# First head pair of a causal attention turned by halves of the tokens

## The chip, the cores and the metric

One core of a Trainium2 chip runs the whole program. The metric is device time in microseconds (us) of one execution. Engines: TensorE (PE, with its weight loads as PEld), VectorE (DVE), ScalarE (ACT), GpSimd (POOL) and SyncE (SP), which issues the DMAs.

## What is computed

```python
def reference(**kwargs):
    ...
    attn_out = _attn_ref(**attn_kwargs)          # q, k, v: (2, 12, 448, 64) float32
    x = np.ascontiguousarray(attn_out.transpose(0, 2, 1, 3)).reshape(B * S, H * D)
    x = _moe_ref(x=x, **moe_kwargs)              # (silu(x @ w_gate) * (x @ w_val)) @ w_out
    return _moe2_ref(x=x, **moe2_kwargs)         # h = x @ w_in; (h * clip(h + 3, 0, 6) / 6) @ w_out

def _attn_ref(q, k, v):
    scores = scale * np.matmul(q, k.transpose(0, 1, 3, 2))
    mask = np.triu(np.ones((seq, seq), dtype=bool), k=1)
    scores = np.where(mask, -1000000000.0, scores)
    scores = scores - np.max(scores, axis=-1, keepdims=True)
    attn = np.exp(scores)
    attn = attn / (np.sum(attn, axis=-1, keepdims=True) + 1e-09)
    return np.matmul(attn, v).astype(np.float32)
```

## The kernel before

`attention()` takes the 24 heads as 12 pairs; the two heads of a pair lie side by side on the 128 rows of a tile (2 x 64). Tokens are cut into four chunks of 112. After the attention, `mlps()` runs the two gated layers, which take the rest of the span.

For one pair, q and k come into `nat` tiles, are turned so that the head's 64 numbers lie along the rows, and are split into a rounded part and a remainder (`qh`, `ql`, `kh`, `kl`; the products are three matmuls, kh with qh, kl with qh and kh with ql). Pairs 0 and 1 (`BY_PE = 2`) are turned on TensorE, four transposes for q and four for k (tiles `tr`); ACT then copies the rounded part out (`CAST kh<-tr`) and DVE subtracts it for the remainder (`kl<-tr,kh`). The later pairs are turned on DVE (`STREAM_TRANSPOSE f<-nat`) and split on POOL, ACT and DVE.

Scores (`sc`) are made in groups of query chunks, `GROUPS = ((2,), (0, 1), (3,))`: chunk c needs keys 0 to c only, so it is (c + 1) x 112 wide, with 224 as the least. DVE adds the mask, scales and takes the extreme value (`e<-sc,mask`, with `m`), ACT takes the exponential (`e<-e,m`) with its row sum, TensorE turns the exponentials (`tp`, ten transposes a head), ACT or DVE copies them out (`et`), and TensorE multiplies them with v (`pv`).

The order on each engine is not written by hand. Every step is handed to a `Plan` (`op`) with a cost per engine that may do it, with what it reads and writes; `Plan.run` then places the steps one by one by their earliest start and by due times worked back from the sum of TensorE's costs. A step with several possible engines is placed on one of them there. The program order that comes out is kept on every engine, so a changed cost, start time (`AT_START`) or step ahead changes the placing of later steps too.

Three places matter below. `load_rows(p)` (L392) issues four loads for pair p on SP, one for each of k and q and each head, 112 rows by four chunks. `busy(n)` issues n matmuls of zeros, 512 columns wide (tile `zero`), which compute nothing that is used; `IDLE = (6, 1, 3, 4)` says how many at the start, after k's turning, after q's, and as filling between the first steps. `first_turn()` (L511) turns pair 0:

```python
for src in (k, q):
    box, parts = rows_turned(0, src)
    got.append(box)
    for part in parts:
        part()
    busy(IDLE[1] if src is k else IDLE[2])
(tk, nk), (tq, nq) = (box["tr"] for box in got)
load(3, k)
load(3, q)
split_bank(0, k, tk, {"act": 0.44})
split_bank(0, q, tq, {"act": 0.44})
```

Of the kernel before, what the change touches and what calls it, by code (L numbers as in the profile page):

```python
# [8 lines left out]
F32 = mybir.dt.float32  # L9
# [5 lines left out]
ALU = mybir.AluOpType  # L15
# [34 lines left out]
BY_PE = 2  # L50
# [2 lines left out]
SOON = 6.0  # L53
CASTS = ("pool", "act")
HOLD, HEAD, LEND = 0.1, 3.0, 0.0
AT_START = {"act": 2.0, "vec": 1.3, "pool": 2.0, "pe": 1.2, "sp": 0.3}
GROUPS = ((2,), (0, 1), (3,))
IDLE = (6, 1, 3, 4)


class InOrder:
# [149 lines left out]
def tile_attention_glu_mlp(  # L211
# [114 lines left out]
    def attention():  # L326
        with ExitStack() as st:
# [21 lines left out]
            def take(kind, n, shape, dt=F32, ready=0.0):  # L349

                i = count[kind] = count.get(kind, -1) + 1
                tag = f"{kind}{i % n}"
                return Spot(lambda: wk.tile(shape, dt, tag=tag, name=kind), (wk, tag), ready=ready)

            def bank(use):
                n = idle.pop(0)
                return Spot(lambda: banks.tile([128, 512], F32, tag=f"bank{n}", name=use), (banks, n)), n
# [3 lines left out]
            def busy(n):  # L361
                for _ in range(n):
                    op(
                        {"pe": 0.38},
                        lambda e: e.matmul(idler(), zeros[:, :128], zeros, start=True, stop=True), writes=[idler],
                    )
# [22 lines left out]
                        writes=[(t, row)], wire=0.6 if rows == 64 else 0.53, soon=SOON,  # L389
                    )  # L390

            def load_rows(p):  # L392

                for src in (k, q):
                    n = (natq if src is q else natk)[p] = take("nat", NAT, [128, NB * D])
                    for j in range(2):
                        op(
                            {"sp": 0.5},
                            lambda e, n=n, j=j, src=src: e.dma_start(
                                out=rows_of(n)[:, :, j, :], in_=src[0, 2 * p + j].rearrange("(c p) d -> p c d", p=C)  # L400
                            ),
                            writes=[(n, j)], wire=0.62,
                        )

            def rows_of(n):
                return n()[:C, : NC * 2 * D].rearrange("p (c j d) -> p c j d", c=NC, j=2)
# [15 lines left out]
            def move(e, out, src):  # L422
                return (e.copy if e.engine is nc.scalar else e.tensor_copy)(out, src)
# [17 lines left out]
            def parts_for(p, src):  # L441
                return sets(p)[:2] if src is q else sets(p)[2:]
# [14 lines left out]
            def split_bank(p, src, t, by):  # L457

                hi, lo = parts_for(p, src)
                op(by, lambda e: move(e, hi(), t()[:, :S]), reads=[t], writes=[hi])  # L460
                op(
                    {"vec": 0.65},
                    lambda e: e.tensor_tensor(out=lo(), in0=t()[:, :S], in1=hi().bitcast(F32), op=ALU.subtract),
                    reads=[t, hi], writes=[lo],
                )

            def rows_turned(p, src):

                n = (natq if src is q else natk).pop(p)
                box = {}  # L470

                def one(c):
                    if c == 0:
                        box["tr"] = bank("tr")
                    op(
                        {"pe": 0.1},
                        lambda e: e.transpose(
                            box["tr"][0]()[:, c * C : (c + 1) * C], rows_of(n)[:, c].rearrange("p j d -> p (j d)"),
                            ident[:C, :C],
                        ),  # L480
                        reads=[n], writes=[box["tr"][0]], kind="tr",
                    )

                return box, [lambda c=c: one(c) for c in range(NC)]
# [25 lines left out]

            def first_turn():  # L511

                got = []
                for src in (k, q):
                    box, parts = rows_turned(0, src)
                    got.append(box)
                    for part in parts:
                        part()
                    busy(IDLE[1] if src is k else IDLE[2])
                (tk, nk), (tq, nq) = (box["tr"] for box in got)  # L520
                load(3, k)
                load(3, q)
                split_bank(0, k, tk, {"act": 0.44})
                split_bank(0, q, tq, {"act": 0.44})
                idle.extend((nk, nq))

            def sc_parts(p):

# [7 lines left out]
                def products(group):  # L536
# [21 lines left out]
                    for cs, terms_ in steps:  # L558
                        op(
                            {"pe": len(terms_) * sum(0.005 + places[c][1] * 0.00044 for c in cs)},  # L560
                            lambda eng, cs=cs, terms_=terms_: work(eng, cs, terms_),
                            reads=[x for i in terms_ for x in terms[i]], writes=[sp for sp, _ in got], kind="sc",
                        )
                    for j, (sp, bn) in enumerate(got):
                        e, m = es[j], ms[j]
# [18 lines left out]
                            )  # L584
                        idle.append(bn)

                return [lambda g=g: products(g) for g in GROUPS]

            def tp_parts(p):

# [203 lines left out]
                    for part in parts:  # L794
                        part()

            for p in range(BY_PE):
                load_rows(p)
            load_v(0)
            load(2, k)  # L800
            load(2, q)
# [825 lines left out]
```

## Time and profile before

| | us |
|---|---|
| median of three runs | 549.36 (549.36, 546.77, 549.46) |
| the profiled execution, whole | 548.23 |
| its span in the profile | 546.5 |
| TensorE busy in it | 536.7 (98%) |
| DVE, ACT, POOL busy | 433.8, 418.8, 196.2 |

The span runs from the first to the last recorded instruction; 1.7 us of the execution lie around it. "Idle before, releaser" in a row names what an engine waited for just before that row. Matmuls overlap, so a row's duration is longer than its distance to the next one. The column PEclk of the stretches is the granted TensorE clock as a share of full speed.

### The profile page before, as it was taken

The numbers are of one execution on the slowest core, as the hardware profiler recorded it, in microseconds if no ns is written. First come the engines' busy times: TensorE is split into PE (matmuls) and PEld (weight loads), VectorE is DVE, ScalarE is ACT, GpSimd is POOL, SyncE is SP. The second block draws the span as 40 slices with busy tenths as digits, with TensorE's granted clock in tenths as the row PEclk, the third lists the DMA queues.
The fourth block names the chain that finished last, engine by engine and source line by source line (L and its number), as shares of the span: only waits on it lengthen the run. The fifth ranks groups of instructions, "written<-read, shape, count | busy, mean of one in ns | idle before, by whom it ended". The sixth has DMA issues, their size and how long they took to land.

```text
span 546.5 us, 8943 instructions
## 1 busy us (share of the span) xinstructions
PE 536.7 (98%) x3107; PEld 486.6 (89%) x3108; DVE 433.8 (79%) x852; ACT 418.8 (77%) x873; POOL 196.2 (36%) x212
## 2 busy tenths in 40 slices
PE   8999999999999999999999999999999999999997
PEld 4677767898999999999999999999999999999997
DVE  5999999899776677699985778777767867599983
ACT  5999986768878778589879877898887847686550
POOL 1798997403232342232020154432333610000511
PEclk9999999999999999999999999999999999999999
DMA  7987713155454544311015444534541066510112
GB/s 204 252 224 213 149 59 116 59 175 172 130 197 137 172 132 158 117 58 59 1 59 185 146 129 122 170 115 132 163 170 58 1 176 215 186 58 2 58 44 101
DMA packets 60236, 69.31 MB, mean 127 GB/s; under 512 B 16928, under 2 KB 54048, under 8 KB 60192
## 3 DMA queue, kind: packets, MB, share of 16 engines
q1 hardware_dynamic: 60192, 68.76, 41.6%
q8 instruction: 24, 0.39, 0.3%
q14 instruction: 20, 0.16, 0.1%
HBM read 65.99 MB, written 2.75 MB: 126 GB/s over the span
## 4 chain that ended last, share of the span: by engine, by line
PE 84%; DVE 11%; DMA 2%; POOL 1%; ACT 1%; issue 1%; POOLq 0%
PE mm L70 73%; PE sc L70 4%; PE pv L70 3%; PE tp L70 3%; DVE op L70 2%; DVE out L70 1%; DVE w L70 1%; PE tr L70 1%; DMA raw<-in_moe_w_gate_dram 1%; DVE e L70 1%; PE zero L70 1%; DVE v L70 1%; DVE et L70 1%; DVE ws L70 1%; DVE t L70 1%
## 5 line engine op out<-in xcount | busy, mean ns | idle before, releaser
L70 PE MATMUL mm<-x,a 128*128 128x448 f32 x396 | 86.3, 365 | 0.0
L70 PE MATMUL mm<-x,s 128*128 128x448 f32 x378 | 81.0, 365 | 0.0
L70 PEld LDWEIGHTS mm<-x,a 128*128 128x128 f32 x396 | 74.4, 188 | 5.9
L70 PEld LDWEIGHTS mm<-x,s 128*128 128x128 f32 x378 | 71.0, 188 | 5.6
L70 ACT ACTIVATE raw<-raw,half 128x768 uint32<-128x768 uint8 x64 | 63.9, 1001 | 0.0
L70 PE MATMUL mm<-t,s 128*128 128x448 f32 x270 | 58.2, 366 | 1.3 <-ACT mm L70 1.3
L70 PE MATMUL mm<-op 128*128 128x384 f32 x315 | 56.6, 335 | 0.3 <-DVE out L70 0.3
L70 PEld LDWEIGHTS mm<-t,s 128*128 128x128 f32 x270 | 50.6, 188 | 5.7 <-ACT mm L70 1.7
L70 PEld LDWEIGHTS mm<-op 128*128 128x128 f32 x315 | 54.7, 188 | 0.9 <-ACT op L70 0.6
L70 ACT ACTIVATE e<-e,m 112x224 f32<-112x224 f32 (+3 forms) x96 | 49.7, 538 | 3.1 <-DVE m L70 3.1
L70 POOL TENSOR_TENSOR a<-w,a 128x384 fp32r<-128x384 f32 x22 | 23.4, 1062 | 72.1 <-ACT a L70 71.3
L70 PE MATMUL mm<-go,wo 128*128 128x448 f32 x189 | 38.9, 366 | 0.0
L70 DVE SCALAR_TENSOR_TENSOR v<-v,raw 128x768 uint32<-128x768 uint32 x34 | 33.9, 1000 | 6.0 <-ACT raw L70 5.9
L70 PEld LDWEIGHTS mm<-go,wo 128*128 128x128 f32 x189 | 35.4, 188 | 3.2 <-ACT mm L70 0.4
L70 ACT ACTIVATE w<-raw 128x768 f32<-128x768 f32 x34 | 31.0, 911 | 8.4 <-DMA raw<-in_moe_w_out_dram 5.5
L70 DVE CUSTOM_DVE_ANT_0 e<-sc,mask 112x112 f32<-112x112 f32 (+3 forms) x96 | 36.5, 437 | 1.1 <-PE sc L70 1.1
L70 DVE SCALAR_TENSOR_TENSOR w<-w,raw 128x768 uint32<-128x768 uint32 x30 | 29.0, 968 | 10.2 <-ACT raw L70 10.2
L70 ACT COPY tmp<-mm 128x448 f32<-128x448 f32 x45 | 23.8, 532 | 12.8 <-PE mm L70 12.5
L70 ACT ACTIVATE v<-raw 128x768 f32<-128x768 f32 x34 | 30.6, 906 | 2.0 <-DMA raw<-in_moe_w_out_dram 1.2
L70 PE MATMUL mm<-x,ws 128*128 128x448 f32 x144 | 30.9, 369 | 0.3 <-POOL x L70 0.3
L70 PEld LDWEIGHTS mm<-x,ws 128*128 128x128 f32 x144 | 26.5, 188 | 2.9 <-POOL x L70 0.7
L70 PE MATMUL tp<-keep,e 112*112 112x112 f32 x240 | 26.4, 261 | 2.7 <-ACT e L70 1.6
(264 smaller groups left out, 1298.5 us busy)
## 6 DMA issues: line engine op xcount, KB each, us to landing
raw<-in_moe_w_out_dram SPq DMA_DIRECT2D x28, 768.0 KB, 4.3
raw<-in_moe_w_in_dram SPq DMA_DIRECT2D x16, 768.0 KB, 4.6
raw<-in_moe_w_gate_dram SPq DMA_DIRECT2D x12, 768.0 KB, 4.4
raw<-in_moe_w_val_dram SPq DMA_DIRECT2D x12, 768.0 KB, 4.2
v<-in_v_dram SPq DMA_DIRECT2D x12, 224.0 KB, 4.7
out_dram<-out SPq DMA_DIRECT2D x14, 192.0 KB, 1.9
nat<-in_k_dram SPq DMA_DIRECT2D x10, 216.0 KB, 4.5
nat<-in_q_dram SPq DMA_DIRECT2D x10, 216.0 KB, 4.8
```

The costliest lines, as they stand in the source:

```text
L70: ins = call(*args, **kw)
```

## The change

Pair 0 is loaded in two halves of the tokens (chunks 0 and 1, then 2 and 3). The first half of q is issued on ACT's queue, the rest on SP's, so pair 0 takes six loads on SP and two on ACT where it took four on SP. Each half of k and of q has its own `tr` bank, its own ACT copy and its own DVE subtraction (224 columns each). The score steps of pair 0 wait for the halves that they read, and its groups come in the order of the chunks: (0, 1), (2,), (3,). `IDLE` falls from 14 zero matmuls to 7, and the planner is told that ACT starts at 0.8 in place of 2.0. Pair 1 is loaded as before, behind pair 0.

```diff
-AT_START = {"act": 2.0, "vec": 1.3, "pool": 2.0, "pe": 1.2, "sp": 0.3}
+AT_START = {"act": 0.8, "vec": 1.3, "pool": 2.0, "pe": 1.2, "sp": 0.3}
-IDLE = (6, 1, 3, 4)
+IDLE = (6, 0, 0, 1)
...
-            def load_rows(p):
+            def load_rows(p, cs, where):
                 for src in (k, q):
-                    n = (natq if src is q else natk)[p] = take("nat", NAT, [128, NB * D])
+                    nats = natq if src is q else natk
+                    if p not in nats:
+                        nats[p] = take("nat", NAT, [128, NB * D])
+                    n = nats[p]
                     for j in range(2):
                         op(
-                            {"sp": 0.5},
+                            {where[src is q]: 0.5},
                             lambda e, n=n, j=j, src=src: e.dma_start(
-                                out=rows_of(n)[:, :, j, :], in_=src[0, 2 * p + j].rearrange("(c p) d -> p c d", p=C)
+                                out=rows_of(n)[:, cs, j, :],
+                                in_=src[0, 2 * p + j].rearrange("(c p) d -> p c d", p=C)[:, cs],
                             ),
-                            writes=[(n, j)], wire=0.62,
+                            writes=[(n, (j, cs.start))], wire=0.155 * (cs.stop - cs.start),
                         )
...
+                for h in range(2):
+                    for src in (k, q):
+                        n = (natq if src is q else natk)[0]
+                        tr, bn = got[h, src is q] = bank("tr")
...
+                        op(
+                            {"pe": 0.25}, work, reads=[(n, (j, 2 * h)) for j in range(2)], writes=[tr], kind="tr",
+                        )
+                        busy(IDLE[1 + h])
+                        hi, lo = parts_for(0, src)
+                        cut = slice(2 * h * C, 2 * (h + 1) * C)
+                        op(
+                            {"act": 0.27}, lambda e, hi=hi, tr=tr, cut=cut: move(e, hi()[:, cut], tr()[:, : 2 * C]),
+                            reads=[tr], writes=[(hi, h)],
+                        )
...
-                return [lambda g=g: products(g) for g in GROUPS]
+                return [lambda g=g: products(g) for g in (sorted(GROUPS) if p == 0 else GROUPS)]
...
-            for p in range(BY_PE):
-                load_rows(p)
+            load_rows(0, slice(0, 2), ("sp", "act"))
+            load_rows(0, slice(2, 4), ("sp", "sp"))
+            load_rows(1, slice(0, 4), ("sp", "sp"))
```

The order of the instructions, first on TensorE from the end of the first run of zero matmuls. Before:

```order
L70 MATMUL tr<-keep,nat 128x112 x4
L70 LDWEIGHTS zeros
L70 MATMUL zero<-zeros 128x512
L70 LDWEIGHTS zeros
L70 MATMUL zero<-zeros 128x512
L70 MATMUL tr<-keep,nat 128x112 x4
L70 LDWEIGHTS zeros
L70 MATMUL zero<-zeros 128x512
L70 LDWEIGHTS zeros
L70 MATMUL zero<-zeros 128x512
L70 MATMUL tr<-keep,nat 128x112 x2
L70 MATMUL sc<-kh,qh 112x336 x2
```

And with the change:

```order
L70 MATMUL tr<-keep,nat 128x112 x6
L70 MATMUL sc<-kh,qh 112x224 x2
L70 MATMUL sc<-kl,qh 112x224 x2
L70 MATMUL sc<-kh,ql 112x224 x2
L70 MATMUL sc<-kh,qh 112x224 x2
L70 MATMUL sc<-kl,qh 112x224 x2
L70 MATMUL tr<-keep,nat 128x112 x2
L70 MATMUL sc<-kh,ql 112x224 x2
L70 MATMUL tr<-keep,nat 128x112 x4
L70 MATMUL sc<-kh,qh 112x448 x2
L70 MATMUL sc<-kl,qh 112x448 x2
L70 MATMUL sc<-kh,qh 112x336 x2
```

The first six transposes are two of k, two of q and two of q's second half; the next two are k's second half, and the next four are all of k of pair 1. One zero matmul fewer stands ahead of them (seven for eight), and none between them. The four transposes of pair 1's k, which stood between the scores of three chunks, now stand in one piece ahead of the scores of chunks 2 and 3.

ACT from its first instruction, before:

```order
L70 ACT_TABLE_LOAD
L70 CAST kh<-tr 128x448
L70 CAST qh<-tr 128x448
L70 CAST kh<-tr 128x448
L70 ACTIVATE e,s<-e,m 112x336 x2
L70 ACTIVATE e,s<-e,m 112x112
L70 CAST qh<-tr 128x448
L70 ACTIVATE e,s<-e,m 112x448
L70 ACTIVATE e,s<-e,m 112x224
```

And with the change:

```order
L70 DMA nat<-in_q_dram 112x2x64 x2
L70 ACT_TABLE_LOAD
L70 CAST kh<-tr 128x224
L70 CAST qh<-tr 128x224 x2
L70 CAST kh<-tr 128x224
L70 ACTIVATE e,s<-e,m 112x112 x2
L70 CAST kh<-tr 128x448
L70 ACTIVATE e,s<-e,m 112x224 x2
L70 CAST qh<-tr 128x448
L70 ACTIVATE e,s<-e,m 112x448
L70 ACTIVATE e,s<-e,m 112x336
```

The last CAST of either list is the rounded part of pair 1's q. Three exponentials of pair 0 stood ahead of it, and four stand there now; behind it come, as before, two exponentials of the first head of pair 0.

SP from its first load, before:

```order
L70 DMA nat<-in_k_dram 112x4x64 x2
L70 DMA nat<-in_q_dram 112x4x64 x2
L70 DMA nat<-in_k_dram 112x4x64 x2
L70 DMA nat<-in_q_dram 112x4x64 x2
L70 DMA nat<-in_k_dram 64x864
```

And with the change:

```order
L70 DMA nat<-in_k_dram 112x2x64 x2
L70 DMA nat<-in_q_dram 112x2x64 x2
L70 DMA nat<-in_k_dram 112x2x64 x2
L70 DMA nat<-in_k_dram 112x4x64 x2
L70 DMA nat<-in_q_dram 112x4x64 x2
L70 DMA nat<-in_k_dram 64x864
```

The loads of pair 1, and every load behind them, stand two places later in SP's queue.

## Rows read from the trace of the kernel before

**Rows 1.** The page: the span and the busy time of each engine.

```profile
span 546.5 us, 8943 instructions
PE 536.7 (98%) x3107; PEld 486.6 (89%) x3108; DVE 433.8 (79%) x852; ACT 418.8 (77%) x873; POOL 196.2 (36%) x212
```

**Rows 2.** Busy time by stretches: stretch, length, engines, PEclk, DMA share, GB/s.

```profile
11.00:12.00 1.00, 0.00 (x0) 0.00 (x0) 1.00 (x4) 1.00 (x5) 0.00 (x0) 1.00 0.92 231
...
20.00:40.00 20.00, 20.00 (x204) 15.13 (x200) 19.66 (x77) 19.84 (x69) 17.86 (x25) 1.00 0.91 228
...
80.00:100.00 20.00, 18.75 (x125) 15.21 (x125) 17.83 (x43) 10.73 (x29) 14.41 (x17) 1.00 0.34 106
100.00:120.00 20.00, 19.67 (x97) 17.95 (x96) 17.38 (x28) 17.50 (x31) 4.37 (x4) 1.00 0.35 113
120.00:140.00 20.00, 18.68 (x92) 16.99 (x92) 19.03 (x31) 15.32 (x29) 5.95 (x5) 1.00 0.42 138
140.00:546.00 406.00, 402.62 (x2074) 379.90 (x2072) 308.60 (x503) 303.66 (x551) 110.54 (x99) 1.00 0.36 116
```

**Rows 3.** The chain of work, 0 to 140 us: start, length, what.

```profile
1.19 3.58 PE zero L70 x8
4.77 0.38 PE tr L70 x4
5.16 0.43 PE zero L70 x2
...
6.60 0.56 PE sc L70 x3
...
10.52 0.53 ACT qh L70
11.06 1.13 ACT e L70 x4
...
13.02 1.27 PE sc L70 x18
```

**Rows 4.** Timeline of ACT: start, length, operation, idle before and its releaser.

```profile
0.73 1.28 ACT L70 ACT_TABLE_LOAD   x1 [0.73 <-PEq L1611]
5.19 0.53 ACT L70 CAST kh<-tr 128x448 fp32r<-128x448 f32 x1 [3.18 <-PE tr L70]
...
8.65 0.57 ACT L70 ACTIVATE e<-e,m 112x336 f32<-112x336 f32 x1 [0.57 <-DVE m L70]
...
9.78 0.37 ACT L70 ACTIVATE e<-e,m 112x112 f32<-112x112 f32 x1
...
13.10 0.47 ACT L70 ACTIVATE e<-e,m 112x224 f32<-112x224 f32 x1
...
16.13 0.60 ACT L70 ACTIVATE e<-e,m 112x336 f32<-112x336 f32 x1
```

**Rows 5.** Timeline of SP: the loads as issued.

```profile
0.73 0.92 SPq L70 DMA_DIRECT2D nat<-in_k_dram  x2
1.70 1.02 SPq L70 DMA_DIRECT2D nat<-in_q_dram  x2
2.76 1.02 SPq L70 DMA_DIRECT2D nat<-in_k_dram  x2
3.83 1.02 SPq L70 DMA_DIRECT2D nat<-in_q_dram  x2
```

**Rows 6.** DMA issues, 0.7 to 1.1 us: count, KB each, us to landing.

```profile
nat<-in_k_dram SPq DMA_DIRECT2D x1, 112.0 KB, 2.3
```

**Rows 7.** DMA issues, 4.85 to 5.4 us (begun before it, the last of pair 1).

```profile
nat<-in_q_dram SPq DMA_DIRECT2D x1, 112.0 KB, 3.4
```

**Rows 8.** Timeline of TensorE, 12 to 17 us.

```profile
12.23 0.79 PE L70 MATMUL tp<-keep,e 112*112 112x112 f32 x6 [1.43 <-ACT e L70]
...
14.22 1.46 PE L70 MATMUL tp<-keep,e 112*112 112x112 f32 x13
15.95 0.46 PE L70 MATMUL sc<-kh,qh 64*112 64x448 f32 x2 [0.28 <-DVE m L70]
```

**Rows 9.** Timeline of DVE: the first remainder, and the first two turnings of pair 2.

```profile
5.76 0.62 DVE L70 TENSOR_TENSOR kl<-tr,kh 128x448 fp32r<-128x448 f32 x1 [4.58 <-ACT kh L70]
...
12.43 1.78 DVE L70 STREAM_TRANSPOSE f<-nat 128x448 f32<-128x448 f32 x2
```

More of the change, by code (lines that the diff above doesn't have):

```diff
@@ L511, in first_turn, with work @@
             def first_turn():
[L513 to L520, printed above, removed]
+                got = {}
+                for h in range(2):
+                    for src in (k, q):
+                        n = (natq if src is q else natk)[0]
+                        tr, bn = got[h, src is q] = bank("tr")
+                        def work(eng, n=n, tr=tr, h=h):
+                            for i in range(2):
+                                eng.transpose(
+                                    tr()[:, i * C : (i + 1) * C],
+                                    rows_of(n)[:, 2 * h + i].rearrange("p j d -> p (j d)"), ident[:C, :C],
+                                )
[8 more added lines that the diff above has]
+                            reads=[tr], writes=[(hi, h)],
+                        )
+                        op(
+                            {"vec": 0.38},
+                            lambda e, hi=hi, lo=lo, tr=tr, cut=cut: e.tensor_tensor(
+                                out=lo()[:, cut], in0=tr()[:, : 2 * C], in1=hi()[:, cut].bitcast(F32), op=ALU.subtract
+                            ),
+                            reads=[tr, (hi, h)], writes=[(lo, h)],
+                        )
+                        idle.append(bn)
+                natq.pop(0), natk.pop(0)
                 load(3, k)
                 load(3, q)
-                split_bank(0, k, tk, {"act": 0.44})
-                split_bank(0, q, tq, {"act": 0.44})
-                idle.extend((nk, nq))
             def sc_parts(p):
@@ L561, in products @@
                             lambda eng, cs=cs, terms_=terms_: work(eng, cs, terms_),
-                            reads=[x for i in terms_ for x in terms[i]], writes=[sp for sp, _ in got], kind="sc",
+                            reads=[
+                                x for i in terms_ for c in cs
+                                for x in (
+                                    (terms[i][0], c // 2), *((terms[i][1], h) for h in range(1 + (c > 1)))
+                                )
+                            ],
+                            writes=[sp for sp, _ in got], kind="sc",
                         )
```

## The prediction

> **What bounds the kernel now.** I read the page first. TensorE is busy for 536.7 of the 546.5 us [rows 1], so what can be won without removing its work is the 9.8 us in which it does nothing. The stretches say where those lie: none from 20 to 40 us, where ACT (19.84 of 20) and DVE (19.66) are as full as TensorE; 2.9 us from 80 to 140 us (1.25, 0.33 and 1.32); 3.4 us in the 406 us behind that [rows 2]. The rest lies in the first 16 us: 1.19 us before the first matmul [rows 3], and the whole microsecond from 11 to 12 us in which TensorE does nothing [rows 2]. The reader should see that the change touches only this start, so its direct worth is a microsecond or two of 548.
>
> The chain shows what the start consists of. Eight zero matmuls hold TensorE to 4.77 us; then come k's four transposes (0.38 us), two zero matmuls (0.43 us) and so on; the first score stands at 6.60 us [rows 3]. Then the chain leaves TensorE: it goes through ACT's copy of pair 1's q at 10.52 us and two exponentials of pair 0 (1.13 us) [rows 3], for which the transposes at 12.23 us waited 1.43 us [rows 8]. From there on TensorE runs nearly through, with one more wait of 0.28 us at 15.95 us [rows 8]. So the moment that counts is not the first score but **the start of that copy on ACT, 10.52 us**, and what lies ahead of it: ACT's own queue, and the landing of pair 1's q.
>
> **The change part by part.**
>
> *Zero matmuls, seven fewer.* One stands ahead of the first transposes: 3.58 us for eight is 0.45 us each [rows 3], so the turning may start at 4.77 - 0.45 = 4.32 us. Four stood between the turnings, at 0.43 us a pair [rows 3], 0.86 us on the path to the first score. The last two stood beside the wait before 12.23 us and are worth nothing.
>
> *Loads.* SP issues a pair of loads in 0.92 to 1.02 us and starts the next pair 1.06 us later [rows 5], 0.53 us a load. The two halves of k go out at 0.73 and 1.2 us. A load lands 2.3 us [rows 6] to 3.4 us [rows 7] after its issue, so the second is there between 3.5 and 4.6 us; the nearest row is the very first load, 2.3 us, with nothing queued, so I take 3.5 to 4.0 us and no wait at 4.32 us. The two that move to ACT stand ahead of its table load; by SP's 0.53 us each they delay it from 0.73 to 1.8 us, so it ends at 3.1 us in place of 2.0. ACT sat idle for 3.18 us until its first copy at 5.19 us [rows 4]; over 1.4 us of cover is left even for a first copy at 4.6 us.
>
> *First score.* Two transposes of k (half of 0.38 us), or twice that if TensorE is still in its slower start, let ACT begin at about 4.6 us. A copy of 448 columns takes 0.53 us [rows 4]; one of 224 lies between 0.27 and 0.53, and I take 0.35 us, since part of it is fixed. Two of them end at 5.3 us, and the first score stands at 5.4 us, 1.2 us earlier. The split copies add 4 x 0.35 - 2 x 0.53 = 0.34 us to ACT. On DVE a remainder of 448 columns takes 0.62 us [rows 9]; four halves between 0.31 and 0.62 us, taken as 0.36, add 0.2 us, beside the 4.58 us that DVE had waited [rows 9].
>
> *ACT's own queue to the copy of pair 1's q.* The second half of k is SP's fifth and sixth load, issued by 3.3 us, and lands between 5.6 and 6.7 us; its transposes and its copy stand ahead of the first exponential, which I put between 6.5 and 7.5 us: 7.0 us, against 8.65 us [rows 4]. Then come two exponentials of 112 (0.37 us [rows 4]), the copy of pair 1's k (0.54 us, from 10.52 to 11.06 us in the chain [rows 3]) and two exponentials of 224 (0.47 us [rows 4]): 2.2 us. By its own queue ACT reaches the copy at **9.2 us**.
>
> *Landing of pair 1's q.* This speaks against the change. The loads of pair 1 stand two places, 1.06 us, later: the last is issued at 4.36 + 1.06 = 5.42 us and lands 2.3 to 3.4 us on, at 7.7 to 8.8 us, where it landed at 7.76 us before (4.36 plus 3.4 [rows 5, 7]). Behind it TensorE has four transposes (0.38 us) and four score matmuls of chunk 2 (0.07 to 0.19 us each, by 1.27 us for 18 and 0.56 us for three [rows 3]; 0.4 us), and the result needs 0.3 us: 8.8 to 9.9 us, in the middle **9.3 us**. That is later than 9.2 us, so I take it: the copy starts 1.2 us earlier than now.
>
> *Behind the copy.* Two exponentials stand there as before, but 448 and 336 wide in place of 448 and 224 (0.57 in place of 0.47 us [rows 4]): 0.1 us is given back, and the wait of the transposes ends at 11.1 us in place of 12.23.
>
> *What of it is carried on.* TensorE carries the 1.1 us, and up to 0.28 us more if the wait at 15.95 us goes, 1.4 us at best. ACT carries less. In the new order it takes all six copies of pair 0's turned exponentials where DVE took one of them; one costs about as much as the other copy of 448 columns, 0.53 us [rows 4], so the first exponential of pair 1, at 16.13 us [rows 4], may come only 0.6 us earlier. ACT is as full as TensorE behind that [rows 2]. Between 0.6 and 1.4 us I take 1.0 us, since TensorE has a little buffer of its own there. DVE's first turnings of pair 2, at 12.43 us [rows 9], wait for loads that come 1.06 us later; the nearest row for one is 3.4 us to landing [rows 7]. Issued by SP's 0.53 us each, the first three are there by 11 us and the last by 12, about when DVE, a microsecond earlier, wants them. Nothing is taken for that.
>
> *Placing of later steps.* From 16 to 75 us only the order of score groups changes, the work of each engine is the same, and all three are full: 0. From 80 to 140 us the planner moves four copies of weights from POOL to ACT and two copies of attention sums back. TensorE idles 2.9 us there and DVE is busy 17.4 to 19.0 of each 20 us [rows 2]; at most those 2.9 us can be won, and I bound the loss by the same. Nothing favours either, so 0, with 1.5 us to each side kept for the range. Behind 140 us the order is the same.
>
> **Sum.** 548.23 - 1.0 = 547.2 us against the profiled execution's own time. The median of the three runs lies 1.1 us above that execution, and the runs spread over 2.7 us; from the median the sum is 548.4 us. I take the middle, **547.8 us**. A measurement of this kernel can tell about 0.5%, 2.7 us, from no change; 1.0 us is under that.
>
> **The rivals.**
>
> *More than the start.* The whole of the two waits goes (1.43 and 0.28 us) and the new placing wins half of the 2.9 us from 80 to 140 us: 3.2 us, 546.2 us from the median. For it: three engines are full in the attention, so one that is earlier drags the others along, and DVE loses two subtractions at the end of the attention. Against it: the loads of pair 1 stand in the way of the first. Chance 0.27.
>
> *The gain is swallowed.* Pair 1's q lands at 8.8 us, its copy starts at 9.9 us, 0.6 us earlier, and ACT's extra copy takes 0.5 us of it: 549.3 us. The change would do what it says for pair 0 and nothing for the end. Chance 0.16.
>
> *TensorE's clock, slower than before.* The column PEclk says 1.00 throughout, but the first eight zero matmuls stand 0.45 us apart and later ones 0.215 [rows 3]; 512 columns in those times are the levels of 1.2 and 2.4 GHz. Before the rise TensorE had done nothing but zero matmuls, back to back. The change leaves seven, then transposes and short scores with gaps. If the lower level held, the work from 4.3 to 16.7 us, 12.4 us less the two waits (1.7 us) and six zero matmuls (1.3 us), 9.4 us, would take twice that, 6 us beyond the present end: 555 us. Up to about 9 us the doubling only fills waits and eats the gain; it makes the kernel slower by over 2.7 us if it lasts past some 13 us. Against it: the rise came by 4.77 us in any case, the wait of 1.43 us did not undo it (the 18 score matmuls behind it took 1.27 us, 0.07 each [rows 3]), and the first transposes come only 0.45 us earlier. The Trainium skill (TensorE: Matmul & The Clock Gate, PE-mode transpose) says that transposes do not count as TensorE being busy for its clock; by that rule the removed zero matmuls were what raised it, and the time would be this rival's 555 us. No row here shows TensorE with transposes alone for long enough to decide it. Chance 0.05, and 0.03 more for a loss of over 2.7 us in the new placing at the end of the attention: 0.08 slower.
>
> **How the numbers follow.** The forecast itself has 0.49. Within 0.5% lie the forecast and the swallowed gain: 0.65; faster 0.27; slower 0.08. The range reaches from 545.0 us (the first rival with most of the 2.9 us) to 550.5 us (no gain at the start, and 1.1 us lost in the new placing).
>
> **What would show it.** Right: seven zero matmuls, the first transposes at about 4.3 us, the first score at 5.4 us, the first exponential at 7.0 us, the copy of pair 1's q at 9.3 us with TensorE as its releaser, the transposes' wait ending at 11.1 us, ACT's first exponential of pair 1 at 15.1 to 15.5 us, and from there the same stretches, 1 us earlier. Wrong: scores of pair 0 that stand twice as far apart as now; the copy of pair 1's q later than 10 us; a new wait of DVE for pair 2's loads; over 4 us or under 1.5 us of idle TensorE from 80 to 140 us.

## The result and the profile after

The changed kernel takes 550.63 us (median of 11 runs, 548.86 to 553.8) against 547.94 us for the kernel before (11 runs, 546.52 to 549.46). The medians lie 2.7 us apart (0.5%); the ratio estimated from all runs of both kernels is 1.0065, 95% interval 1.0045 to 1.0086. (The ratios below are estimated in the same way, so they need not equal the quotient of two medians.) The change makes the kernel slower, where 547.8 us and a range up to 550.5 had been forecast. The profiled execution took 550.34 us, with a span of 548.5.

The page of the changed kernel, beside [rows 1]:

```profile
span 548.5 us, 8944 instructions
PE 539.3 (98%) x3101; PEld 489.0 (89%) x3101; DVE 435.1 (79%) x853; ACT 421.4 (77%) x879; POOL 198.0 (36%) x209
```

TensorE does seven zero matmuls fewer and is busy 2.6 us longer, with a span 2.0 us longer: it is not its waiting that has grown. The chain shows where the work at the start became longer (start, length, what), beside [rows 3]:

```profile
4.35 0.76 PE tr L70 x4
...
5.53 0.99 PE sc L70 x10
...
6.87 0.33 PE sc L70 x2
...
7.31 0.28 DVE e L70
...
13.46 2.19 PE sc L70 x14
```

The start is as forecast up to the first score: turnings from 4.35 us, first score at 5.53 in place of 6.60. ACT's rows, beside [rows 4], agree (start, length, operation, idle time before it and its releaser):

```profile
1.70 1.28 ACT L70 ACT_TABLE_LOAD   x1 [1.70 <-PEq L1643]
4.76 0.35 ACT L70 CAST kh<-tr 128x224 fp32r<-128x224 f32 x1 [1.78 <-PE tr L70]
...
7.62 0.39 ACT L70 ACTIVATE e<-e,m 112x112 f32<-112x112 f32 x1 [0.38 <-DVE m L70]
...
10.48 0.53 ACT L70 CAST qh<-tr 128x448 fp32r<-128x448 f32 x1 [0.64 <-PE tr L70]
```

ACT takes its first copy 0.43 us earlier and its first exponential 1.03 us earlier. Then the gain is lost: the copy of pair 1's q stands at 10.48 us (before 10.52) and the transposes that wait for the exponentials at 12.28 (before 12.23). Behind that wait the same 18 score matmuls take 2.19 us where they took 1.27 (the chain counts 14 of them; TensorE's timeline has all 18, from 13.39 us on). The stretches say why: stretch, length, busy time of PE, PEld, DVE, ACT and POOL, then the granted clock, DMA share, GB/s:

```profile
11.00:12.00 1.00, 0.00 (x0) 0.00 (x0) 1.00 (x6) 1.00 (x4) 0.00 (x0) 1.00 1.15 210
12.00:13.00 1.00, 0.72 (x4) 0.72 (x5) 1.00 (x3) 1.00 (x5) 0.00 (x0) 0.53 0.91 243
13.00:14.00 1.00, 1.00 (x7) 0.71 (x7) 0.71 (x1) 1.00 (x4) 0.41 (x2) 0.50 1.01 349
14.00:16.00 2.00, 2.00 (x22) 1.85 (x19) 1.26 (x7) 0.66 (x2) 1.91 (x3) 0.63 1.11 248
...
84.00:86.00 2.00, 2.00 (x13) 2.00 (x12) 2.00 (x7) 0.81 (x2) 1.17 (x2) 0.50 0.04 12
```

And before, behind the same empty microsecond [rows 2]:

```profile
12.00:13.00 1.00, 0.77 (x8) 0.62 (x8) 1.00 (x4) 1.00 (x5) 0.00 (x0) 1.00 0.97 343
13.00:14.00 1.00, 1.00 (x17) 1.00 (x18) 1.00 (x2) 1.00 (x6) 0.55 (x1) 1.00 0.94 241
```

TensorE's clock fell to 0.50, its lower level of 1.2 GHz, right behind the empty microsecond from 11 to 12 us, and again just before 84 us. Before, it stayed at 1.00 in both places. TensorE's own rows, with idle time and its releaser, show both places and what they make of the time, first in the changed kernel, then before:

```profile
12.28 1.18 PE L70 MATMUL tp<-keep,e 112*112 112x112 f32 x5 [1.65 <-ACT e L70]
...
16.96 0.46 PE L70 MATMUL sc<-kh,qh 64*112 64x448 f32 x2
...
80.91 0.85 PE L70 MATMUL mm<-x,ws 128*128 128x448 f32 x3 [1.08 <-ACT ws L70]
...
82.78 0.57 PE L70 MATMUL tp<-keep,e 112*112 112x112 f32 x4 [0.47 <-ACT rs L70]
83.83 2.46 PE L70 MATMUL tp<-keep,e 112*112 112x112 f32 x12 [0.48 <-DVE m L70]
...
123.15 1.99 PE L70 MATMUL mm<-x,a 128*128 128x448 f32 x9
128.62 1.98 PE L70 MATMUL mm<-x,a 128*128 128x448 f32 x9
```

```profile
80.55 0.57 PE L70 MATMUL tp<-keep,e 112*112 112x112 f32 x4 [0.59 <-DVE m L70]
81.60 1.40 PE L70 MATMUL tp<-keep,e 112*112 112x112 f32 x12 [0.48 <-DVE m L70]
...
119.41 1.99 PE L70 MATMUL mm<-x,a 128*128 128x448 f32 x9
...
124.54 2.08 PE L70 MATMUL mm<-t,s 128*128 128x448 f32 x9 [1.32 <-ACT mm L70]
126.46 1.98 PE L70 MATMUL mm<-x,a 128*128 128x448 f32 x9
```

The last of pair 1's first score groups ("the last group" below), which stood at 15.95 us [rows 8], stands at 16.96: 1.0 us late. Near the end of the attention TensorE is idle three times, 2.03 us in all (before, 0.59, 0.48 and, at 87.00 us, 0.22 us), and the second fall follows (12 transposes in 2.46 us; before, 12 took 1.40). The rows `mm<-x,a` are the first and the second product with an expert's weights behind the attention; I use them as marks. Before, they started at 119.41 and 126.46 us, with a wait of 1.32 us between them; now at 123.15 and 128.62 without one. So 2.16 us of loss are left at the second mark, and the span is 2.0 us longer.

### The profile page after: what moved, and what is told of

Same layout as the page of the kernel before. It is cut to its first block, busy times and chain, and to the rows that moved or that the text cites. A ratio compares the mean times of both kernels' runs of the same rounds, so it can differ in the third digit from the quotient of the medians.

```text
span 548.5 us, 8944 instructions
## 1 busy us (share of the span) xinstructions
PE 539.3 (98%) x3101; PEld 489.0 (89%) x3101; DVE 435.1 (79%) x853; ACT 421.4 (77%) x879; POOL 198.0 (36%) x209
## 4 chain that ended last, share of the span: by engine, by line
PE 92%; DVE 6%; ACT 0%; POOL 0%; issue 0%; DVEq 0%
PE mm L70 78%; PE sc L70 4%; PE pv L70 4%; PE tp L70 4%; DVE op L70 2%; PE tr L70 1%; DVE out L70 1%; DVE w L70 1%; PE zero L70 1%; DVE e L70 1%; DVE v L70 1%; POOL rb L70 0%; ACT e L70 0%; DVE et L70 0%; DVE mm L70 0%
## 5 line engine op out<-in xcount | busy, mean ns | idle before, releaser
L70 PE MATMUL tp<-keep,e 112*112 112x112 f32 x240 | 27.6, 269 | 2.6 <-ACT e L70 1.6
```

Of the source, the lines that this page charges most:

```text
L70: ins = call(*args, **kw)
```

## The experiments

Two causes stood to be told apart, and a third question was the missing gain. **A:** the removed zero matmuls had kept the clock up over the wait. **D:** the new placing at the end of the attention costs time. Each version's ratio is against the kernel before, timed beside it (its median there lay between 547.74 and 549.33 us). Marks are of the profiled execution, clock is the number of timed executions whose mean granted clock was 0.997 or less. It was so in 9 of 11 executions of the changed kernel, and in none of 134 of before (three more, of 662 to 1882 us, one of them at a clock of 0.754, are in no ratio). Three versions that are not in the table have their numbers in the text; their clock count is 0 of 12 each.

| version | median us | ratio, 95% | marks us | clock |
|---|---|---|---|---|
| before, last two zeros out | 549.17 | 1.0018 (0.9993 to 1.0043) | 121.62, 127.20 | 10 of 12 |
| before, seven zeros out | 548.84 | 1.0004 (0.9978 to 1.0031) | 124.29, 129.96 | 7 of 12 |
| before, eight more | 547.88 | 1.0001 (0.9978 to 1.0024) | 119.30, 124.90 | 0 of 12 |
| changed + two zeros | 550.37 | 1.0038 (1.0017 to 1.0059) | 123.27, 128.74 | 5 of 9 |
| changed + eight | 549.45 | 1.0019 (0.9994 to 1.0045) | 122.97, 128.44 | 8 of 12 |
| changed, old last 290 steps | 549.67 | 1.0013 (0.9989 to 1.0037) | 120.45, 127.45 | 6 of 12 |
| eight + last 290 | 547.80 | 0.9991 (0.9970 to 1.0013) | 118.97, 125.65 | 0 of 12 |
| eight + two casts back | 549.54 | 1.0038 (1.0023 to 1.0053) | 122.53, 128.11 | 9 of 11 |
| eight + three weight steps back | 551.17 | 1.0047 (1.0021 to 1.0074) | 122.71, 128.18 | 10 of 10 |
| eight + last 100 | 546.24 | 0.9955 (0.9924 to 0.9986) | 118.79, 124.26 | 0 of 10 |
| changed, old last 100 steps | 548.06 | 0.9993 (0.9965 to 1.0021) | 120.26, 125.73 | 9 of 12 |
| eight + last 100 + k's turning | 545.73 | 0.9941 (0.9913 to 0.9969) | 118.23, 123.81 | 0 of 12 |

The zero matmuls put in stand directly ahead of the first transposes of pair 0's exponentials, that is, in the wait (one version has four more at the start); the order of everything else is kept. The diffs show the lines that matter; those that count the zero matmuls and the steps are left out.

**The last two zero matmuls alone (b_no_last2).**

```diff
+                if kind == "zero" and seen[kind] in (13, 14):
+                    return
```

> The kernel before without its last two zero matmuls, which stand in the wait ahead of 12.23 us; nothing else changed. The prediction gave them no worth: time as before, 18 scores behind the wait in 1.27 us. Theory A gives them the clock: the granted clock falls in the wait (0.5 to 0.7 between 12 and 16 us), the 18 scores take 2.0 to 2.5 us, the last of pair 1's first groups stands 0.8 to 1.1 us later than 15.95 us, and the median is up by 0.5 to 1.5 us. Rival Z (only the seven together, with those between the turnings, matter): start and time as before.

The stretches of this version, columns as above:

```profile
12.00:13.00 1.00, 0.39 (x3) 0.39 (x4) 1.00 (x3) 1.00 (x5) 0.00 (x0) 0.85 1.03 311
13.00:14.00 1.00, 1.00 (x8) 0.71 (x6) 1.00 (x4) 1.00 (x7) 0.00 (x0) 0.50 0.99 234
14.00:16.00 2.00, 2.00 (x18) 1.90 (x18) 1.30 (x3) 1.36 (x4) 1.79 (x3) 0.50 1.20 236
```

TensorE's rows at the wait and at the last group:

```profile
12.61 1.33 PE L70 MATMUL tp<-keep,e 112*112 112x112 f32 x6 [1.41 <-ACT e L70]
...
17.83 0.46 PE L70 MATMUL sc<-kh,qh 64*112 64x448 f32 x2 [0.28 <-DVE m L70]
```

The fall comes in the kernel before, with no other edit; the 18 scores stand from 13.87 to 16.10 us, 2.23 us. The mechanism is A's, and Z falls. The wait is 1.41 us long, no longer than before's 1.43 [rows 8]: so its length alone does not explain the fall; what is missing are the two zero matmuls ahead of it. The last group is 1.88 us late, more than A's 0.8 to 1.1, since 0.38 us are lost ahead of the wait already: the first transposes ran longer here (four in 0.95 us, before in 0.58). The second mark is 0.74 us late; the wait of 1.32 us that before has between the marks is gone. The interval of the ratio still includes 1.

**All seven (b_7zeros).** The same edit with numbers 8 to 14.

> The kernel before with its own plan kept on every engine, but zero matmuls 8 to 14 (one ahead of the first transposes, four between the turnings, two in the wait behind pair 1's q) not issued. Theory A, the removed zero matmuls let TensorE's clock fall: granted clock about 0.5 from some 12 to 15 us although nothing is loaded by halves, the 18 score matmuls behind the wait take over 2 us in place of 1.27, the last pair 1 score group starts 0.5 to 1 us later than 15.95 us, time 1.001 to 1.004 of before. Theory B, the halves and their waits are the cause: clock 1.00 throughout, start 0 to 0.5 us earlier, ratio 0.998 to 1.000.

The median did not move, and the profiled execution fits neither theory. It shows another clock trouble, at the start (TensorE's timeline):

```profile
4.15 2.44 PE L70 MATMUL tr<-keep,nat 112*128 112x112 f32 x10
...
18.20 2.68 PE L70 MATMUL tp<-keep,e 112*112 112x112 f32 x13
20.80 0.47 PE L70 MATMUL sc<-kh,qh 64*112 64x448 f32 x2
```

13 transposes in 2.68 us, against 1.46 [rows 8]: the clock did not rise before about 20.8 us, though the column says 1.00 throughout (it shows a fall, not a late first rise). The start without those zeros has a clock that differs from execution to execution, and a look at one of them does not price it.

**Two put back in the changed kernel (a_fill2), and eight (a_fill8).**

```diff
+                if kind == "tp" and seen[kind] == 1:
+                    for _ in range(2):
+                        by["pe"].matmul(idler(), zeros[:, :128], zeros, start=True, stop=True)
```

> The changed kernel with only two zero matmuls put back, the two that before stood ahead of the wait that ended at 12.23 us; all else as changed. Theory A2 (those two alone hold the clock over the wait): granted clock 1.00 from 8 to 20 us, 18 scores behind the wait in 1.25 to 1.35 us, last of pair 1's first groups at 15.5 to 16.1 us in place of 16.96; the tail keeps its own fall; median 0.5 to 1.5 us under the changed kernel's 550.63. Rival B2 (the change lost more than those two, the four between the turnings matter as much): the clock still falls between 12 and 16 us, last group later than 16.5 us.

TensorE's timeline with two:

```profile
12.28 0.69 PE L70 MATMUL tp<-keep,e 112*112 112x112 f32 x5 [1.21 <-ACT e L70]
...
15.56 0.46 PE L70 MATMUL sc<-kh,qh 64*112 64x448 f32 x2
```

One of its stretches, columns as above:

```profile
13.00:14.00 1.00, 1.00 (x18) 1.00 (x18) 1.00 (x2) 1.00 (x4) 0.41 (x2) 1.00 0.90 325
```

The clock stays at 1.00 from 8 to 20 us, the wait is still 1.21 us long, and the last group stands 1.40 us earlier than in the changed kernel and 0.39 earlier than before. So these two alone do it, A2 holds, and the four between the turnings aren't needed for it. The mark at the end of the attention did not move (123.27): the microsecond is lost again there, and the median, 0.26 us under the changed kernel's, misses the 0.5 to 1.5 us expected.

> The changed kernel with its own plan kept, and eight zero matmuls issued right ahead of the first transposes of exponentials, in the wait from 10.5 to 12.3 us. Theory A (clock at the start): granted clock 1.00 from 10 to 18 us, pair 1's last score group starts at 15.7 to 16.0 us in place of 16.96, span 1.0 us shorter than the changed kernel, ratio to before about 1.004, the rest lying at 79 to 90 us. Theory B (clock falls for another cause than the missing zero matmuls): fall and time as in the changed kernel, 1.0065. Theory C (the whole loss hangs on the start): 1.000 or less.

Clock 1.00 from 8 to 20 us here too (A), last group at 16.03 us; the span is only 0.1 us shorter than the changed kernel's, not 1.0. At the end of the attention the second fall is longer than in the changed kernel, 0.55, 0.50 and 0.50 in the three stretches from 82 to 88 us; the middle one:

```profile
84.00:86.00 2.00, 2.00 (x11) 1.91 (x10) 2.00 (x6) 1.09 (x3) 2.00 (x2) 0.50 0.00 0
```

**Eight in the kernel before (b_fill8).** The same edit there.

> The kernel before, its order kept, with eight zero matmuls more ahead of the first transposes of pair 0's exponentials (the wait of 1.43 us that ended at 12.23 us). Theory A (it is the empty microseconds of TensorE that let its clock fall or rise late): before's own runs above 549 us become rarer, the median falls by 0 to 1.5 us, the profiled start is unchanged (last scores of pair 1's first groups at 15.9 to 16.1 us). Rival R (the runs above 549 us come from the first rise of the clock, ahead of 10 us, or from elsewhere): no change of the median beyond 0.3%.

No change of the median: more zero matmuls than before's two bring nothing there. Its runs of over 549 us stayed (3 of 12), as R has it.

**Eleven at the start (a_fill8_tail_z4).** Four more ahead of the first turning, on top of eight in the wait and the last 290 steps as before (an edit shown below).

```diff
+                if kind == "zero" and seen[kind] == 1:
+                    for _ in range(4):
+                        by["pe"].matmul(idler(), zeros[:, :128], zeros, start=True, stop=True)
```

> The changed kernel with eight zero matmuls in the wait and the old placing at the end of the attention, and four zero matmuls more at the very start (eleven in place of seven). Theory F (runs 2 to 3 us longer of one and the same kernel are runs in which TensorE's clock rises late at the start): the longer group of runs (549 to 550.3 us) gets rarer; the start is 0.9 to 1.8 us later, so the short group stands at 548.2 to 549.2 us. Rival G (the longer runs come from elsewhere): the two groups stay, both 0.9 to 1.8 us up.

548.48 us, 1.0016 (0.9994 to 1.0037). The two groups of runs stayed (7 up to 548.5 us, 5 from 549.47), as in the version without the four (5 of 12 from 549.05), so nothing speaks for F: that the spread of 2 to 3 us within one kernel comes from the first rise is not shown. The start is 0.92 us later and the span 0.6.

**The end of the attention put back (a_tail290, a_fill8_tail).** The times and engines that the planner gives the last 290 steps are replaced by those of the kernel before:

```diff
-            plan.run(lambda t, engine, call: call(by[engine]))
+            plan.run(lambda t, engine, call: call(by[engine]), TAIL)
```

> The changed kernel, its start unchanged, with the last 290 steps of the attention (from about 50 us on) placed on the engines and in the order of the kernel before. Theory D (the new placing at the end of the attention makes waits and a second fall of the clock, 1.2 us of the loss): no stretch under 0.9 of the clock from 80 to 90 us, idle TensorE there 1.3 us as before, ratio 1.002 to 1.004, the fall at 12 to 15 us remains. Rival (the second fall follows from the start's shift in time, whatever the placing): it stays, 1.0065.

D holds: the fall at the start is there (0.50 from 13 to 14 us), that behind 80 us is gone, and the first mark is 2.7 us earlier than in the changed kernel. The ratio, 1.0013, is under the 1.002 to 1.004 expected.

> Both edits at once: eight zero matmuls in the wait, and the last 290 steps placed as before. If A and D together are the whole loss: the time of the kernel before, ratio 0.999 to 1.001, no stretch with a low clock, and no gain left, since the copy of pair 1's q starts at 10.48 us against 10.52. If a gain of the halves is hidden behind the two losses: 0.996 to 0.999.

Both causes taken away give 547.80 us, and the interval of the ratio includes 1: A and D are the loss. That leaves which of the 290 steps it is.

**Two casts of weights back on POOL (a_fill8_casts).** The diff names steps by their numbers in the attention's plan, with planned times in us and engines; the two are the casts w to ws at 77.28 and 80.37 us.

```diff
+SOONER = {481: 74.82, 485: 74.85}
+OTHER = {481: 'pool', 485: 'pool'}
```

Where the reason lies is seen on DVE and POOL in the changed kernel. DVE's timeline:

```profile
76.75 3.59 DVE L70 SCALAR_TENSOR_TENSOR w<-raw,w 128x384 uint32<-128x384 uint32 x2
```

POOL's:

```profile
76.96 0.77 POOL L70 COPY rb<-r 112x512 f32<-112x512 f32 x1 [0.46 <-DVE r L70]
77.69 1.13 POOL L70 TENSOR_TENSOR x<-xa,x 128x448 fp32r<-128x448 f32 x1
78.78 1.14 POOL L70 TENSOR_TENSOR xa<-xa 128x448 f32<-128x448 f32 x1
```

One of these two DVE operations takes 3.16 us, where the median of the four between 66 and 92 us is 0.55: it ends at 80.34 us, 0.42 us after the last of POOL's three (79.92). ACT's cast waits for it (1.91 us, at 80.37) and TensorE for that.

> The changed kernel with eight zero matmuls in the wait at 10.3 us, its own placing at the end of the attention kept but for two steps: the two casts of weights that it makes on ACT (77.3 and 80.4 us) stand on POOL again, ahead of its three operations of 0.8 to 1.1 us there. Theory T (DVE's second split of the weights takes 3.16 us in place of 0.55 because it stands beside POOL's three operations, and the cast that waits for it on ACT holds up TensorE and the exponentials behind it): that split takes 0.5 to 1.1 us, TensorE's wait ahead of these weights' product falls from 1.08 us to under 0.4, the clock falls no more between 80 and 92 us, the first product of the part behind the attention stands at 118.8 to 119.8 us in place of 122.97, the span is 545.4 to 546.4 us. Rival U (the two casts are not the cause; the other steps that the planner moved are): TensorE's three waits keep 1.5 us or more, the clock falls, the first product stands at 121.5 us or later.

DVE's timeline of this version, and then TensorE's:

```profile
77.23 3.03 DVE L73 TENSOR_TENSOR ws<-w,ws 128x384 fp32r<-128x384 f32 x1
```

```profile
80.32 0.47 PE L73 MATMUL mm<-x,ws 128*128 128x448 f32 x1 [1.46 <-DVE ws L73]
```

The split is quick now (two in 1.48 us), but the next DVE operation with two inputs takes 3.03 us beside POOL instead, and TensorE waits 1.46 us for it. The loss is handed on, not removed: T falls. This execution shows no fall of the clock; 9 of its 11 timed ones do.

**A third weight step (a_fill8_ws3).** One remainder too is on POOL, as before.

```diff
+SOONER = {481: 74.82, 485: 74.84, 482: 74.86}
+OTHER = {481: 'pool', 485: 'pool', 482: 'pool'}
```

> The changed kernel with eight zero matmuls in the wait at 10.3 us, and of its placing at the end of the attention three steps undone: the two casts of weights and one of their two remainders stand on POOL, as before. Theory X (the first loss at the end of the attention is that both remainders stand on DVE, one of them stalled to 3.03 us beside POOL's operations while TensorE waits 1.46 us for it): no wait of TensorE for weights between 77 and 82 us over 0.3 us, the first product of the part behind the attention at 120.5 to 121.6 us in place of 122.5 to 123. Rival Y (the loss sits in the steps behind 80 us): that product at 122 us or later.

TensorE's timeline:

```profile
81.85 3.51 PE L73 MATMUL tp<-keep,e 112*112 112x112 f32 x16 [2.15 <-DVE m L73]
```

No wait for weights any more, but the masks behind the held DVE operation (3.42 us this time) are late, and TensorE waits 2.15 us for them. X falls, and Y's condition holds.

**The last 100 steps back, the weights left as changed (a_fill8_tail100).** The edit of a_fill8_tail, with a table of 100 steps in place of 290 (its planned times are all 0.13 us later than in that table).

> The changed kernel with eight zero matmuls in the wait at 10.3 us, and only the last 100 steps of the attention placed and ordered as before (the weights' steps at 75 to 81 us and the sums' copies at 60 to 75 us stay as changed). Rival Y (the loss sits in the last steps: the copies of the sums and of the last turned exponentials): first product of the part behind the attention at 118.8 to 120 us, no fall of the clock behind 80 us. Theory X (it sits in the weights' steps): TensorE's wait of about 1 us for weights stays, and that product stands at 120.5 us or later.

TensorE's timeline:

```profile
79.30 0.47 PE L72 MATMUL mm<-x,ws 128*128 128x448 f32 x1 [0.58 <-DVE ws L72]
...
118.79 1.99 PE L72 MATMUL mm<-x,a 128*128 128x448 f32 x9
124.26 1.99 PE L72 MATMUL mm<-x,a 128*128 128x448 f32 x9
```

0.9955 (0.9924 to 0.9986): faster than before, and its median is 4.4 us under the changed kernel's. Y holds, though TensorE still waits 0.58 us for weights. In the last 100 steps the masks stand between the weights' steps and POOL's copy for the sums stands earlier, no DVE operation takes over 1.07 us between 74 and 86 us, and the clock does not fall. Which of the 100 steps does it stays open.

**The end mended, the start not (a_tail100).** The same table without the zero matmuls.

> The changed kernel with its own start, no zero matmul added, and only the last 100 steps of the attention as before. Theory A (what the change loses at the start is the clock alone): the clock falls between 12 and 16 us in most runs (mean granted clock 0.996 or 0.997), last of pair 1's first groups at about 16.9 us, about 1 us later through the attention, median 1 to 2 us above the version with zero matmuls in the wait. Rival N (behind the mended end of the attention the start's microsecond is taken up by a wait): median within 0.4 us of it.

0.9993 against 0.9955, and both marks 1.47 us later; the last group stands at 17.34 us against 15.83. A holds: that is the price of the clock at the start once nothing behind it takes it up. The two intervals overlap; the medians (548.06 and 546.24) and the marks carry the reading.

**The missing gain at the start (a_fill6_tail_q, a_fill8_tail_k).** First the four transposes of pair 1's q are put ahead of the last five score groups of pair 0, with the old last 290 steps and six zeros in the wait.

```diff
+SOONER = {67: 7.86, 76: 7.87, 77: 7.88, 78: 7.89}
```

> The changed kernel with zero matmuls (six) in the wait and the old placing at the end of the attention, and also the four transposes of pair 1's queries ahead of the last five score groups of pair 0 on TensorE in place of among and behind them. Theory Q (the missing start gain is TensorE's order: those transposes stand behind scores that wait for a bank and for the remainder of k's second half): the copy of pair 1's q starts at 9.7 to 9.9 us in place of 10.48, the wait ends at 11.5 to 11.8 us in place of 12.28, the last of pair 1's first groups stands at 14.9 to 15.3 us, profiled span 544.8 to 545.3 us, median 0.5 us under the version without that move. Rival L (it is the landing of pair 1's q, or the masks of chunk 3 on DVE): the copy moves by under 0.3 us, or the wait ends at 12.0 us or later.

ACT's timeline of this version:

```profile
9.62 0.52 ACT L74 CAST qh<-tr 128x448 fp32r<-128x448 f32 x1
10.57 0.67 ACT L74 ACTIVATE e<-e,m 112x448 f32<-112x448 f32 x1 [0.44 <-DVE m L74]
```

The copy comes 0.87 us earlier than with the old order and gains nothing (L): the exponential behind it waits for DVE, and the last group stands at 15.68 us, where it stood at 15.57 without the move (a_fill8_tail). 549.22 us, 1.0009 (0.9988 to 1.0030). Then the transposes of k's second half are put behind chunk 1's last scores:

```diff
+SOONER = {31: 6.26}
```

> The changed kernel with zero matmuls in the wait and the old placing at the end of the attention, and the transposes of k's second half (pair 0) put behind the last two score matmuls of chunk 1 in place of ahead of them. Theory V (what bounds the start now is DVE's queue, which begins with the first mask at 7.31 us, and that waits for chunk 1's last matmul since chunks 0 and 1 share one bank): the first mask starts at 6.9 to 7.05 us, DVE's first turning of pair 2 at 11.6 to 11.75 us in place of 11.99, the last of pair 1's first groups at 15.2 to 15.35 us in place of 15.57. Rival W (it is k's second half, its copy on ACT and its remainder, that bounds): the mask starts earlier, but the last of pair 1's first groups stands at 15.5 us or later.

DVE's timeline of this version, then TensorE's:

```profile
6.79 0.27 DVE L74 CUSTOM_DVE_ANT_0 e<-sc,mask 112x112 f32<-112x112 f32 x1 [0.50 <-PE sc L74]
...
11.66 1.75 DVE L74 STREAM_TRANSPOSE f<-nat 128x448 f32<-128x448 f32 x2
```

```profile
15.24 0.46 PE L74 MATMUL sc<-kh,qh 64*112 64x448 f32 x2
```

The mask starts 0.52 us earlier and the last group 0.33 us. V holds: in this version an earlier first mask on DVE makes an earlier end of the start. 547.63 us, 1.0003 (0.9986 to 1.0020): with the old last 290 steps a wait of 1.40 us ahead of the second mark takes it back.

**Both mended parts together (a_fill8_tail100_k).**

> Both mended parts together: the changed kernel with eight zero matmuls in the wait, the transposes of k's second half behind chunk 1's last score matmuls, and the last 100 steps of the attention as before. Theory S (the gains add up, since the earlier start is carried to the end of the attention when TensorE's clock holds): last of pair 1's first groups at 15.3 to 15.6 us, first product of the part behind the attention at 118.3 to 118.7 us, its second at 123.7 to 124.1 us, median 545.5 to 547 us, ratio to before 0.993 to 0.998. Rival S0 (the third of a microsecond is taken back by a wait at 80 to 125 us, as it was with 290 steps put back): second product at 124.2 us or later, median within 0.2 us of the version without the moved transposes (546.24 us).

545.73 us, 0.9941 (0.9913 to 0.9969), marks at 118.23 and 123.81: S holds, the best version here. Its last group at 15.26 us stands 0.69 us ahead of before's. That it beats the version without the moved transposes is seen in the marks and in the last group (15.83 us there, with first scores just as slow in either); the two intervals overlap.

## Why the prediction was wrong

**"The last two stood beside the wait before 12.23 us and are worth nothing": the first step that failed.** They cost no time and were worth the clock: without them the 18 scores take 0.92 us more and the last group comes 1.0 us later than before, 1.4 us later than with two put back. The prediction counted the matmuls that lie on the path and not what an idle TensorE does to the rows behind it. The clock's rival (0.05) had the right engine and the wrong place. It asked when the first rise comes, and argued that the wait of 1.43 us "did not undo it", when two zero matmuls stood right ahead of that wait; with as long a wait and without them, the clock fell (b_no_last2). The Trainium skill (TensorE: Matmul & The Clock Gate, What's actually happening) says that the clock follows how busy TensorE has lately been; the trace agrees, with 0.53 and 0.50 behind the emptied wait and 1.00 with two zeros back. The rule of the Trainium skill (TensorE: Matmul & The Clock Gate, PE-mode transpose) cited ahead of the result, that transposes do not count as busy, would by the prediction's reading have kept the clock low through the turnings. In the profiled execution of the changed kernel, which has no zero matmul between them, the scores from 6.16 us on already stand 0.10 us a pair apart, as close as at 19.58 us; the execution of b_7zeros with its rise at 20.8 us would fit the rule. So the rival's late rise does occur, there and not in the changed kernel's profiled execution.

**"Placing of later steps", taken at "0, with 1.5 us to each side kept for the range": the second.** Put back, these steps are worth 2.7 us at the first mark and 1.2 at the second, where a wait of 1.3 us has come back (290 steps, no zeros), or 4.2 us at both (100 steps, eight zeros). Bounding the loss by TensorE's present idle time, 2.9 us, left out that each wait can also halve the clock behind it: from 80 to 140 us the changed kernel idles 2.2 us, less than before, and is slower all the same. The version with only the end mended is at 0.9993 (100 steps) or 1.0013 (290), against 1.0065: most of the measured loss is this step. The start's microsecond comes on top only where the end does not swallow it, as it does in the changed kernel (second mark 128.62, with two zeros 128.74).

**"The copy starts 1.2 us earlier", 9.3 us: the third.** It stood at 10.48. The landing of pair 1's q, from which the 9.3 us were worked out, did not hold it: its loads were issued from 4.70 us on and took 2.6 and 2.5 us, but its last transposes stand behind scores, at 9.94 us. First came the exponential at 7.62 us, not 7.0: chunks 0 and 1 share one bank, so the first mask waits for chunk 1's last scores at 6.87, which stand behind the transposes of k's second half, and DVE starts at 7.31 us (1.08 us of wait). From there DVE's queue runs nearly full up to pair 2's turning, at 11.98 in place of 12.43 us [rows 9]. Those 0.45 us are what the halves give in this execution; the last group gains 0.39 once the clock holds. Some executions give less: in the six profiled ones with the changed start, its own order there and zeros in the wait, the last group stands between 15.56 and 16.03 us (before 15.95, before with eight more 15.84), latest in those where the first pair of scores still takes 0.53 us in place of 0.36. Taking ACT's copy for the moment that counts was the error, as a_fill6_tail_q shows.

**Right:** the turnings at 4.35 us (4.32), no wait for pair 0's loads, the table load ended at 2.98 us (3.1) with 1.78 us of cover left, the first score at 5.53 (5.4). The range ended at 550.5 because it took a start without gain and 1.1 us of loss; it had no term for a start that loses. The base was also high: the middle of the profiled execution and the median of three runs is 548.8 us, 0.9 above the median of 11; from that median the same gain of 1.0 us gives 546.9.

## What to carry to other kernels

An instruction that fills a wait may be paying for the clock of the work behind it: before removing it, ask what TensorE does right after, and price that work at half the clock. A change in a planner's input reshuffles steps far from the edit; look at those places as at the edit itself, and when the sum is negative, try the new start with the old end. The first engine to be freed is not the bound if the next one's queue starts late: follow the chain through each engine's first instruction.

## What the runs showed that was not expected

- DVE operations with two inputs in SBUF (remainders of weights, 0.55 us alone) took 2.46 us in before and 3.03 to 3.42 in the experiments while POOL ran two or three operations back to back. The Trainium skill (GPSIMD Engine Reference, Specifications) says that POOL shares its SBUF interfaces with VectorE, with contention where a DVE instruction has two SBUF inputs; the trace agrees so far as each of these ends 0.41 us after POOL's last operation (before, 80.09 and 79.68 us). In a_fill8_tail100 two DVE operations with two inputs end as long behind a single operation of POOL and take 0.91 and 1.07 us, though POOL goes on. What decides between the two is open.
- Within most versions runs lie in two groups, 2 to 3 us apart, before's too. Two profiled executions of the longer group had a stretch in which matmuls stood further apart at a granted clock of 1.00: 292 in 60 us in place of 298 (before without its last two zeros, 140 to 200 us), and in before with eight more zeros this stretch (columns as above), with 486 where the kernel before has 495:

```profile
300.00:400.00 100.00, 100.00 (x486) 90.83 (x485) 73.97 (x117) 82.57 (x146) 37.12 (x35) 1.00 0.47 141
```

  A step of 2 us between two single runs of such a kernel says nothing of a change. What causes it stays open.
